# Three-stage attention and feed-forward kernel: weight words of the second phase loaded ahead of their conversions, scratch stores behind the loads

## Chip, cores, metric

One core of a Trainium2 chip. The metric is the device time of one execution in microseconds (us); lower is better. Half a per cent of it is 2.6 us.

## Reference

Three stages in fp32, on 2 x 768 = 1536 tokens of 512 features:

```python
# 1: attention, 8 heads of 64; a window of +-15 keys, and 24 block summaries (max of k, mean of v over 32)
a = softmax(concat(where(near, q @ k.T / 8, -1e9), q @ ksum.T / 8 + log(32)))
x = a @ concat(v, vsum)                       # as [1536, 512]
# 2: feed-forward 512 -> 1024 -> 512
h = x @ w_in
s = h * softmax(h)
x = (s - mean(s)) / sqrt(var(s) + 1e-6) * g_ln @ w_out
# 3: feed-forward 512 -> 2048 -> 512, elu
h = x @ w_in2
out = where(h > 0, h, exp(min(h, 0)) - 1) @ w_out2
```

The weights reach the kernel as 64-bit words (two 32-bit words per number), so each one is converted to fp32 on the chip, and then split into a high and a low part. A product is three matmuls: high times high, high times low, low times high (L103 to L105).

## The kernel before, in words

The program has two phases. **The first** runs stage 1 and stage 2 as one loop over 24 "ticks" (`ticks`): in each, one tile of 64 tokens enters attention (`attn_s`), others are further on (`attn_p`, `attn_x`), half of a product with `w_in` is done for 128 tokens (`mm_in`), and, as they come ready, transposes (`tr`, into `lnT`) and products with `w_out` (`mm_out(i, d)`, 24 matmuls for 384 tokens and 128 features, L103 to L105 with `y_ps`). Behind the ticks stand `mm_out` of the third and of the fourth block of 384 tokens, with the last three transposes. `mm_out` leaves its result in PSUM; ACT copies it into the three tiles `y` of 512 tokens each (L305), and the blocks of 384 don't meet the tiles of 512: a result of the third block goes in part to the second tile and in part (128 tokens) to the third.

**The second phase** is stage 3. First the first 512 tokens: 16 blocks `f` of 128 hidden features, each `ffn2_in(f)` (12 matmuls, `h2`, then the elu and its split into `g_hl`) and, one block behind, `ffn2_out` (12 matmuls into `o_ps`). Then the other 1024 tokens by products of sums (`yf`, `w3e`, `w3l`, `c11`, `c12`, `c21`).

The weights of stage 3 are converted in 32 pieces, 16 of `w_in2` (here ("w3", f)) and 16 of `w_out2` (("w4", f)), half a megabyte of words each. `todo` holds their order, and `more_w(n)` does the next n. One conversion is: a DMA of the words into a buffer (`load_words`, L112); Abs of the high words on ACT (L120); a clamp on POOL (L123); three VectorE steps (L124, L125, L129), of which L125 and L129 read the words too. A `w3` piece stays in SBUF. A `w4` piece is split (ACT L133, VectorE L100) and stored to scratch in DRAM (`store_w4`, L358, `w4d`), from where it is read back three times into the three buffers `w4r` (`load_w4`, L381).

The buffers for the words are pieces of the `y` tiles that don't hold results yet: `spare` is at first two halves of the third `y` tile (in the trace `y<-in_w_in`, in the order below `y2_67`). So the evacuations of `mm_out` into the third tile wait for the last conversions out of it. After the ticks one half of the first tile and two halves of another tile take their place.

All DMAs are issued from SP's queue, which runs in order; while the first phase lasts, their order on SP is that of the program. In `more_w` a `w3` or `w4` piece is loaded, in program order, just ahead of its own conversion, and the stores of earlier pieces are issued ahead of that (`store_w4()` stands before each `more_w`). The order on the other engines is made by a scheduler, also in order at run time; only on TensorE, in the products of sums, it is the program's.

Of the kernel before, what the change touches and what calls it, by code (L numbers as in the profile page):

```python
# [9 lines left out]
F32 = mybir.dt.float32  # L10
F32R = mybir.dt.float32r
BF16 = mybir.dt.bfloat16
I32 = mybir.dt.int32
# [19 lines left out]
TC = 512  # L33
KD, KF1, KF2 = DM // 128, F1 // 128, F2 // 128
# [17 lines left out]
def tile_kernel(ctx: ExitStack, tc: tile.TileContext, qd, kT, v, w_in, w_out, g_ln, w_in2, w_out2,  # L52
# [4 lines left out]
    state = {"late": 0}  # L57
# [10 lines left out]
    stage = [[t.bitcast(I32)[:, i * 1024:(i + 1) * 1024].rearrange("p (k f) -> p k f", k=KD)  # L68
              for i in range(KD * TC // 1024)] for t in flat]

    p_c = ctx.enter_context(tc.tile_pool(name="p_c", bufs=1, side="right"))
    p_ln = ctx.enter_context(tc.tile_pool(name="p_ln", bufs=1, side="right", reuse_waits="tile"))
# [15 lines left out]
    dump = p_ln.tile([128, F1], BF16, tag="dump", name="dump")  # L88
# [22 lines left out]
    def load_words(bits, src):  # L111
        nc.sync.dma_start(bits, src if len(src.shape) == 3 else src.rearrange("p (k f) -> p k f", k=KD))  # L112
# [19 lines left out]
    def split(hi, lo, x):  # L132
        nc.scalar.activation(hi, x, AF.Copy)  # L133
        lo_of(lo, x, hi)

    def convert(bits, src, hi, lo, g=None, pin=False):
        if src is not None:
            load_words(bits, src)
        hi, lo = (t if len(t.shape) == 3 else t.rearrange("p (k f) -> p k f", k=KD) for t in (hi, lo))
        x = to_f32(bits, pin=pin)  # L140
        if g is None:
            split(hi, lo, x)
        else:
            nc.scalar.activation(hi, x, AF.Copy, scale=g)
            nc.vector.scalar_tensor_tensor(lo, x, g, hi.bitcast(F32), op0=ALU.mult, op1=ALU.subtract)
# [45 lines left out]
    def load_v(n):  # L191
        b, t = divmod(n, NT)
        nc.sync.dma_start(vws[n % NBUF][0:WIN, :], v[b, t * TQ:t * TQ + WIN, :])
# [101 lines left out]
    def ffn1_out(i, d, k):  # L295
# [4 lines left out]
        if k == KF1 - 1:  # L300
# [6 lines left out]
                t0 = t1  # L307

    w3t, w3e, w3l, w3_hl, w4s, w4_hl, yhl, yf = {}, {}, {}, {}, {}, {}, {}, {}
    stores, spare = [], [*stage[2]]  # L310
    todo = [("w3", 0), ("w3", 1), ("w4", 0), ("w3", 2), ("w3", 3), ("w4", 1), ("w3", 4), ("w3", 5), ("w4", 2),
            ("w4", 3), ("w3", 6), ("w4", 4), ("w3", 7), ("w4", 5), ("w3", 8), ("w4", 6), ("w3", 9), ("w4", 7),
            ("w4", 8), ("w4", 9)]
    todo += [("w3", f) for f in range(10, KF2)] + [("w4", f) for f in range(10, KF2)]

    def bits():
        state["late"] += 1
        return spare[state["late"] % len(spare)]

    def home(p):  # L320
        if p < 2:
# [10 lines left out]
    def base_of(f):  # L332
        return w3f(f // 2)[:, 2:6:3] if f % 2 else w3f(f // 2)[:, 0:4:3]

    def convert_w3(f):
        b = bits()
        load_words(b, w_in2[:, f * 128:(f + 1) * 128].bitcast(I32).rearrange("(k p) f -> p k f", p=128))
        if f % 2 == 0:
            home(f // 2)
        to_f32(b, base_of(f).bitcast(I32))  # L340
# [5 lines left out]
        nc.vector.tensor_tensor(t[:, 1], t[:, 4], t[:, 0], op=ALU.subtract)  # L346
        nc.vector.tensor_tensor(t[:, 6], t[:, 3], t[:, 1], op=ALU.subtract)

    def convert_w4(f):
        t = w4s[f % 2]  # L350
        tr_ = t.bitcast(F32R)
        convert(bits(), w_out2[f * 128:(f + 1) * 128, :].bitcast(I32), tr_[:, 0], tr_[:, 1])
        stores.append((f, t))

    def store_w4():
        while stores:
            f, t = stores.pop(0)
            nc.sync.dma_start(w4d[f], t.rearrange("p c f -> p (c f)"))  # L358

    def more_w(n=1):  # L360
        for _ in range(n):
            if todo:
                what, f = todo.pop(0)
                (convert_w3 if what == "w3" else convert_w4)(f)

    def plain_w3(f):
        if f < KF2:
# [119 lines left out]
    late = {**dict.fromkeys(range(11, 21), 1), 21: 2, 22: 2, 23: 2}  # L487
    for t, (j, n) in enumerate(ticks):
        s_n, p_n, x_n = t + LEAD, t + LEAD - 2, t + LEAD - 3
        if t == 0:  # L490
            sum_v(1)
        elif t == 1:
            load_k(1)
        elif t == 3:
            sum_k(1)
        if x_n < NU and t:
            load_v(x_n)
        if s_n < NU:
            for u in (s_n + 1, s_n):
                if u < NU and u not in q_bd:  # L500
                    load_q(u)
            load_kw(s_n + 1)
            attn_s(s_n)
        mm_in(j, n)
        if p_n < NU:
            attn_p(p_n)
        for f, *args in after[t]:
            f(*args)
        if x_n < NU:
            attn_x(x_n)  # L510
        for _ in range(fetches.get(t, 0)):
            words.pop(0)()
        for _ in range(converts.get(t, 0)):
            parts.pop(0)()
        store_w4()
        more_w(late.get(t, 0))
        if x_n == NU - 1:
            p_at.release()
            p_w3 = ctx.enter_context(tc.tile_pool(name="p_w3", bufs=1, side="left", reuse_waits="tile"))
            for f in (3, 4):  # L520
                w3t[f] = p_w3.tile([128, 2048], F32, tag=f"f{f}", name="w3f")
            w3e[0] = p_w3.tile([128, 2, 3, 2, 128], F32R, name="w3e")
            last_t = p_w3.tile([128, 2, KF1, TB], F32R, tag="last", name="lnT")
            lnT_last = [last_t[:, c] for c in range(2)]
    p_in.release()
    p_y = ctx.enter_context(tc.tile_pool(name="p_y", bufs=1, side="right", reuse_waits="tile"))
    for d in range(KD):
        mm_out(NJ // 3 - 2, d)
        store_w4()
        if d == 2:  # L530
            split_y(0)
            spare[:] = stage[0][:1]
            mids = [stage[0][1].bitcast(F32).rearrange("p k f -> p (k f)")[:, c * TC:(c + 1) * TC] for c in range(2)]
            more_w()
        if d < 3:
            tr(NJ - 3 + d)
    tb = p_y.tile([128, 2, KD, 256], I32, tag="yc", name="bits")
    spare.extend(tb[:, c] for c in range(2))
    gw = p_w.tile([128, 6, 2, TC], F32R, tag="lnT", name="g_hl")
    wt = p_ln.tile([128, 5, 2, TC], F32R, tag="ln", name="w4r")  # L540
    w4r = [wt[:, c] for c in range(3)]
    w3h = [(t[:, 0], t[:, 1]) for t in (gw[:, 4], gw[:, 5], wt[:, 3], wt[:, 4])]
    for d in range(KD):
        mm_out(NJ // 3 - 1, d)
        store_w4()
        more_w()
        if d > 1:
            plain_w3(d - 2)
    store_w4()
    psh.release()  # L550
    loads.__exit__(None, None, None)
    mids.append(p_ln.tile([128, TC], F32, tag="dump", name="m"))

    pso = ctx.enter_context(tc.tile_pool(name="pso", bufs=4, space=PSUM))
    NTT = TC // 128
# [49 lines left out]
        load_w4(n)  # L605
    ops = tiles_o()
    for f in range(KF2):
        more_w(2)
        store_w4()
        ffn2_in(f)  # L610
        plain_w3(f + 2)
        for t in range(NTT):
            if f:
                ffn2_out(ops, t, f - 1)
        load_w4(f + 2)
        if f == 9:
            t4 = forms_early()
        if f == 12:
            sums_w3(0)
            w3l[0] = p_w.tile([128, 2, 4, 2, 128], F32R, tag="w3", name="w3l")  # L620
            split_w3(0)
            sums_w3(1)
# [23 lines left out]
    for p in range(NP3):  # L646
# [33 lines left out]
        pool, tag = ((p_k, "k") if p < 2 else (p_k, "f2") if p == 2 else (p_w3, f"f{p}") if p < 5 else (p_w, f"w{p - 5}"))  # L680
# [72 lines left out]
```

## Time and profile before

| | us |
|---|---|
| median of 3 runs | 520.16 (518.06 to 520.97) |
| the profiled execution | 520.19 |
| its span, first to last instruction | 518.4 |
| PE (TensorE matmul) busy | 471.9, 91% |
| DVE (VectorE) busy | 330.0, 64% |
| ACT busy | 287.7, 55% |
| POOL busy | 125.8, 24% |
| DMA, mean share of the 16 engines | 48.6% for SP's queue |

The profile is of one execution. A row of its timelines gives the start of an instruction in us from the span's start, its length, engine, line, operation and tiles, and in brackets how long its engine was idle before it and which instruction released it. Matmuls overlap their neighbours: a row's length is more than the spacing of two. The time of the runs is some 1.8 us more than the span.

### The profile page before, as it was taken

The numbers are of one execution on the slowest core, as the hardware profiler recorded it, in microseconds if no ns is written. First come the engines' busy times: TensorE is split into PE (matmuls) and PEld (weight loads), VectorE is DVE, ScalarE is ACT, GpSimd is POOL, SyncE is SP. The second block draws the span as 40 slices with busy tenths as digits, with TensorE's granted clock in tenths as the row PEclk, the third lists the DMA queues.
The fourth block names the chain that finished last, engine by engine and source line by source line (L and its number), as shares of the span: only waits on it lengthen the run. The fifth ranks groups of instructions, "written<-read, shape, count | busy, mean of one in ns | idle before, by whom it ended". The sixth has DMA issues, their size and how long they took to land.

```text
span 518.4 us, 7444 instructions
## 1 busy us (share of the span) xinstructions
PE 471.9 (91%) x2568; PEld 393.2 (76%) x2568; DVE 330.0 (64%) x759; ACT 287.7 (55%) x635; POOL 125.8 (24%) x198
## 2 busy tenths in 40 slices
PE   0988999999999998709999999779999999999997
PEld 1555888889978988709988887558888888888885
DVE  2798879978693769453565699977666666442000
ACT  1776888965773466232554648547766667551001
POOL 2886555872335313110000132300000000000000
PEclk9999999999999999868999999989999999999999
DMA  8986994262444223733347557574211212227654
GB/s 293 364 287 188 283 287 136 61 183 91 148 135 152 66 85 109 243 123 93 111 130 258 180 168 227 213 262 144 82 54 68 82 41 82 82 82 242 196 185 148
DMA packets 40117, 82.47 MB, mean 159 GB/s; under 512 B 9616, under 2 KB 18448, under 8 KB 40080
## 3 DMA queue, kind: packets, MB, share of 16 engines
q1 hardware_dynamic: 40080, 82.00, 48.6%
q8 instruction: 20, 0.33, 0.3%
q14 instruction: 17, 0.14, 0.1%
HBM read 70.46 MB, written 11.53 MB: 158 GB/s over the span
## 4 chain that ended last, share of the span: by engine, by line
PE 64%; DVE 14%; DMA 9%; issue 5%; ACT 3%; POOL 2%; SPq 1%; ACTq 0%; POOLq 0%; DVEq 0%
PE o_ps L105 6%; PE o_ps L104 6%; PE o_ps L103 6%; PE c L104 5%; PE c L105 5%; PE c L103 5%; PE h L103 5%; PE h L105 4%; PE h L104 4%; PE s_ps L213 3%; PE y_ps L103 3%; PE y_ps L104 3%; PE y_ps L105 3%; DMA y<-in_w_in 3%; PE x_ps L249 3%
## 5 line engine op out<-in xcount | busy, mean ns | idle before, releaser
L123 POOL TENSOR_SCALAR conv<-conv 128x512 f32<-128x512 f32 x48 | 40.0, 836 | 136.5 <-ACT conv L120 135.1
L103 PE MATMUL y_ps<-lnT,w_out 128*128 128x384 f32 x128 | 45.1, 353 | 16.2 <-ACT y L305 12.8
L103 PE MATMUL o_ps<-w4r,g_hl 128*128 128x512 f32 x128 | 50.9, 397 | 6.6 <-DMA w4r<-w4d 6.6
L227 POOL TENSOR_SCALAR sm<-sm,st 128x120 f32<-128x120 f32 x96 | 47.6, 513 | 28.6 <-DVE st L225 13.0
L104 PE MATMUL o_ps<-w4r,g_hl 128*128 128x512 f32 x128 | 50.6, 395 | 0.0
L120 ACT ACTIVATE conv<-y 128x512 f32<-128x512 f32 x38 | 25.4, 672 | 44.7 <-DMA y<-in_w_in 33.3
L105 PE MATMUL o_ps<-w4r,g_hl 128*128 128x512 f32 x128 | 48.2, 395 | 0.0
L104 PE MATMUL y_ps<-lnT,w_out 128*128 128x384 f32 x128 | 44.6, 350 | 0.0
L105 PE MATMUL y_ps<-lnT,w_out 128*128 128x384 f32 x128 | 44.5, 350 | 0.0
L124 DVE TENSOR_SCALAR conv<-conv 128x512 int32<-128x512 int32 x48 | 22.3, 464 | 29.7 <-POOL conv L123 29.7
L103 PE MATMUL h<-w_in,xT 128*128 128x512 f32 x96 | 40.2, 419 | 0.8 <-ACT xT L252 0.8
L213 PE MATMUL s_ps<-kw,q_bd 128*128 128x120 f32 x192 | 28.7, 296 | 12.6 <-DMA q_bd<-in_qd 11.7
L105 PE MATMUL h<-w_in,xT 128*128 128x512 f32 x96 | 38.7, 403 | 0.5 <-DVE xT L100 0.5
L222 ACT ACTIVATE sm<-sm,st 128x120 f32<-128x120 f32 x96 | 36.8, 387 | 4.2 <-DVE st L219 2.7
L104 PE MATMUL h<-w_in,xT 128*128 128x512 f32 x96 | 38.3, 399 | 0.6 <-DVE w_in L100 0.6
L103 PEld LDWEIGHTS y_ps<-lnT,w_out 128*128 128x128 f32 x128 | 25.4, 199 | 17.3 <-ACT y L305 13.2
L213 PEld LDWEIGHTS s_ps<-kw,q_bd 128*128 128x128 f32 x192 | 25.1, 203 | 13.9 <-POOL kw L96 11.6
L103 PEld LDWEIGHTS o_ps<-w4r,g_hl 128*128 128x128 f32 x128 | 24.5, 191 | 13.7 <-issue 3.3
L592 DVE COPY y<-o_ps 128x512 f32<-128x512 f32 x5 | 3.4, 689 | 43.5 <-PE o_ps L105 43.5
L594 ACT ACTIVATE y<-o_ps 128x512 f32<-128x512 f32 x6 | 3.6, 598 | 45.1 <-PE o_ps L105 45.1
L105 PEld LDWEIGHTS o_ps<-w4r,g_hl 128*128 128x128 f32 x128 | 24.5, 191 | 5.2
L104 PEld LDWEIGHTS o_ps<-w4r,g_hl 128*128 128x128 f32 x128 | 24.3, 190 | 5.0
(151 smaller groups left out, 1268.2 us busy)
## 6 DMA issues: line engine op xcount, KB each, us to landing
w4r<-w4d SPq DMA_DIRECT2D x48, 512.0 KB, 4.2
y<-in_w_in SPq DMA_DIRECT2D x20, 512.0 KB, 6.2
y<-in_w_out SPq DMA_DIRECT2D x18, 512.0 KB, 5.2
w4d<-w3f SPq DMA_DIRECT2D x16, 512.0 KB, 3.5
q_bd<-in_qd SPq DMA_DIRECT2D x24, 256.0 KB, 6.1
vw<-in_v SPq DMA_DIRECT2D x24, 192.0 KB, 5.7
k_sb<-in_kT SPq DMA_DIRECT2D x8, 400.0 KB, 5.2
v_sb<-in_v SPq DMA_DIRECT2D x12, 256.0 KB, 6.0
```

The source lines that it names most:

```text
L103: nc.tensor.matmul(ps, lhsT=l[0][ls], rhs=r[0][rs], start=first, stop=False, skip_group_check=parts)
L104: nc.tensor.matmul(ps, lhsT=l[0][ls], rhs=r[1][rs], start=False, stop=False, skip_group_check=parts)
L105: nc.tensor.matmul(ps, lhsT=l[1][ls], rhs=r[0][rs], start=False, stop=last, skip_group_check=parts)
L120: first = nc.scalar.activation(x, high.bitcast(F32), AF.Abs)
L123: nc.gpsimd.tensor_scalar(x, x, F64_HUGE, F64_TINY, op0=ALU.min, op1=ALU.max)
L124: nc.vector.tensor_scalar(a, a, 3, 0x3FFFFFF8, op0=ALU.logical_shift_left, op1=ALU.bitwise_and)
L213: nc.tensor.matmul(sps[:, p, 0:KW], lhsT=q_bd[n][:, p, :], rhs=kw[:, p, :], start=True, stop=True)
L222: nc.scalar.activation(sm[:, p, :], sm[:, p, :], AF.Exp, bias=nm[:, p:p + 1], scale=-1.0, accum_out=ss[:, p:p + 1])
L227: nc.gpsimd.tensor_scalar(sm[:, p, :], sm[:, p, :], ri[:, p:p + 1], 1.0, op0=ALU.mult, op1=ALU.mult)
L249: nc.tensor.matmul(xps[ds, p, :], lhsT=vw[:KW, p * 128 + hh * D:p * 128 + (hh + 1) * D], rhs=pT[:KW, p, hh * TQ:(hh + 1) * TQ], start=True ...
L592: nc.vector.tensor_copy(o, ops[t])
L594: nc.scalar.activation(o, ops[t], AF.Copy)
```

## The change

- `fetch()` is new: it loads the words of the next pieces of `todo` as long as fewer than `len(spare) - 1` are waiting for their conversion (`ahead`). It is called first in the tick before the first conversion, then at the head of each `more_w`. With the two buffers of the first phase one load is ahead, with the four later ones three.
- `more_w` now calls `fetch()`, then `store_w4()`, then does the oldest piece of `ahead`. A store of a `w4` piece therefore stands behind the next load. The separate calls of `store_w4` are gone.
- The later buffers are four halves of two tiles (`yc`, `yd`), taken from the second output tile (d = 1) of the third block of 384 tokens on; the first `y` tile holds none any more, and its four quarters are scratch for the elu (`mids`).
- In the third block of 384 tokens two pieces are converted instead of one, in the fourth four as before. In the first 512 tokens of the second phase `more_w()` does one piece per block of 128 features instead of two, and `todo` alternates there between `w4` and `w3`.
- `forms_early` (sums of the other tokens, which take the tiles `yc` and `yd`) stands after block 11 instead of 9.

```diff
-    stores, spare = [], [*stage[2]]
+    stores, ahead, spare = [], [], [*stage[2]]
     todo = [("w3", 0), ("w3", 1), ("w4", 0), ("w3", 2), ("w3", 3), ("w4", 1), ("w3", 4), ("w3", 5), ("w4", 2),
             ("w4", 3), ("w3", 6), ("w4", 4), ("w3", 7), ("w4", 5), ("w3", 8), ("w4", 6), ("w3", 9), ("w4", 7),
-            ("w4", 8), ("w4", 9)]
-    todo += [("w3", f) for f in range(10, KF2)] + [("w4", f) for f in range(10, KF2)]
-
-    def bits():
-        state["late"] += 1
-        return spare[state["late"] % len(spare)]
+            ("w4", 8), ("w4", 9), ("w3", 10), ("w3", 11)]
+    for f in range(10, KF2):
+        todo += [("w4", f)] + [("w3", f + 2)] * (f + 2 < KF2)
+
+    def fetch():
+        while todo and len(ahead) < len(spare) - 1:
+            what, f = todo.pop(0)
+            b = spare[state["late"] % len(spare)]
+            state["late"] += 1
+            if what == "w3":
+                load_words(b, w_in2[:, f * 128:(f + 1) * 128].bitcast(I32).rearrange("(k p) f -> p k f", p=128))
+            else:
+                load_words(b, w_out2[f * 128:(f + 1) * 128, :].bitcast(I32))
+            ahead.append((what, f, b))
...
     def more_w(n=1):
         for _ in range(n):
-            if todo:
-                what, f = todo.pop(0)
-                (convert_w3 if what == "w3" else convert_w4)(f)
+            fetch()
+            store_w4()
+            if ahead:
+                what, f, b = ahead.pop(0)
+                (convert_w3 if what == "w3" else convert_w4)(f, b)
...
-        store_w4()
+        if t == min(late) - 1:
+            fetch()
         more_w(late.get(t, 0))
...
+    tb = [p_y.tile([128, 2, KD, 256], I32, tag=n, name="bits") for n in ("yc", "yd")]
     for d in range(KD):
         mm_out(NJ // 3 - 2, d)
-        store_w4()
+        more_w(d > 1)
+        if d == 1:
+            spare[:] = [t[:, c] for c in range(2) for t in tb]
+            state["late"] = 0
+            fetch()
         if d == 2:
             split_y(0)
-            spare[:] = stage[0][:1]
-            mids = [stage[0][1].bitcast(F32).rearrange("p k f -> p (k f)")[:, c * TC:(c + 1) * TC] for c in range(2)]
-            more_w()
+            mids = [stage[0][h].bitcast(F32).rearrange("p k f -> p (k f)")[:, c * TC:(c + 1) * TC]
+                    for h in range(2) for c in range(2)]
...
     for f in range(KF2):
-        more_w(2)
-        store_w4()
+        more_w()
         ffn2_in(f)
...
-        if f == 9:
+        if f == 11:
             t4 = forms_early()
```

What this does to the order on SP, at the end of the ticks (`y2_67` is the third `y` tile as a buffer, `w4d5_101` the scratch of ("w4", 5)). Before:

```order
L358 DMA w4d4_100<-w3f_1367 128x1024
L112 DMA y2_67<-in_w_in2 128x4x256
L112 DMA y2_67<-in_w_out2 128x1024
L381 DMA w4r_2478<-w4d0_96 128x1024
L381 DMA w4r_2478<-w4d1_97 128x1024
L381 DMA w4r_2478<-w4d2_98 128x1024
L358 DMA w4d5_101<-w3f_1650 128x1024
L112 DMA y2_67<-in_w_in2 128x4x256
L112 DMA y2_67<-in_w_out2 128x1024
```

With the change (`bits` are the new buffers):

```order
L112 DMA y2_67<-in_w_in2 128x4x256
L364 DMA w4d4_100<-w3f_1367 128x1024
L112 DMA y2_67<-in_w_out2 128x1024
L112 DMA y2_67<-in_w_in2 128x4x256
L364 DMA w4d5_101<-w3f_1650 128x1024
L112 DMA y2_67<-in_w_out2 128x1024
L112 DMA bits_2312<-in_w_in2 128x4x256
L112 DMA bits_2313<-in_w_out2 128x1024
L112 DMA bits_2312<-in_w_out2 128x1024
L389 DMA w4r_2490<-w4d0_96 128x1024
L389 DMA w4r_2490<-w4d1_97 128x1024
L389 DMA w4r_2490<-w4d2_98 128x1024
```

Each load now stands ahead of the store that it stood behind, and the last two loads into the third `y` tile (L112 ahead of the first `bits` row) ahead of the three reads of `w4r`.

On ACT, the same place in the program, from the copies of the last 384 tokens' first transposes on (`lnT_2155`; `conv_2253` is ("w3", 7), `conv_2293` ("w3", 8), `conv_2300` ("w4", 6)). Before:

```order
L290 ACTIVATE lnT_2155<-t_ps_2381 128x4x128
L290 ACTIVATE lnT_2155<-t_ps_2388 128x4x128
L133 ACTIVATE w3f_1367<-conv_2216 128x512
L305 ACTIVATE y1_66<-y_ps_2395 128x256
L290 ACTIVATE lnT_2155<-t_ps_2435 128x4x128
L120 ACTIVATE conv_2253<-y2_67 128x512
L290 ACTIVATE lnT_2155<-t_ps_2442 128x4x128
L120 ACTIVATE conv_2260<-y2_67 128x512
L133 ACTIVATE w4r_2478<-w3f_1650 128x512 x2
L305 ACTIVATE y1_66<-y_ps_2449 128x256
L133 ACTIVATE g_hl_2477<-w3f_1367 128x512 x2
L133 ACTIVATE w3f_1650<-conv_2260 128x512
```

With the change:

```order
L290 ACTIVATE lnT_2155<-t_ps_2385 128x4x128
L290 ACTIVATE lnT_2155<-t_ps_2392 128x4x128
L120 ACTIVATE conv_2293<-y2_67 128x512
L133 ACTIVATE w3f_1650<-conv_2260 128x512
L305 ACTIVATE y1_66<-y_ps_2399 128x256
L290 ACTIVATE lnT_2155<-t_ps_2439 128x4x128
L305 ACTIVATE y2_67<-y_ps_2314 128x128
L305 ACTIVATE y2_67<-y_ps_2355 128x128
L290 ACTIVATE lnT_2155<-t_ps_2446 128x4x128
L133 ACTIVATE w4r_2490<-w3f_1650 128x512 x2
L120 ACTIVATE conv_2300<-y2_67 128x512
L120 ACTIVATE conv_2427<-bits_2312 128x512
```

The Abs of ("w3", 8) moved from behind the evacuation of `y_ps_2449` to ahead of that of the tile before, and two evacuations into the third tile now stand ahead of the last transposes' copy.

On ACT earlier, at the end of the first phase (`conv_2140` is ("w4", 3), `conv_2209` ("w3", 6), `conv_2216` ("w4", 4)). Before:

```order
L305 ACTIVATE y0_65<-y_ps_2100 128x128
L305 ACTIVATE y1_66<-y_ps_2100 128x256
L252 ACTIVATE xT_2064<-x_ps_2127 128x4x64
L120 ACTIVATE conv_2140<-y2_67 128x512
L290 ACTIVATE lnT_94<-t_ps_2179 128x4x128
L290 ACTIVATE lnT_94<-t_ps_2186 128x4x128
L270 ACTIVATE ln_95,st_2168<-h_2087,st_2168 128x1024
```

With the change:

```order
L120 ACTIVATE conv_2209<-y2_67 128x512
L305 ACTIVATE y0_65<-y_ps_2100 128x128
L305 ACTIVATE y1_66<-y_ps_2100 128x256
L252 ACTIVATE xT_2064<-x_ps_2127 128x4x64
L120 ACTIVATE conv_2216<-y2_67 128x512
L290 ACTIVATE lnT_94<-t_ps_2179 128x4x128
L290 ACTIVATE lnT_94<-t_ps_2186 128x4x128
```

Each Abs stands one conversion earlier than before among the same evacuations and copies.

## Rows read from the trace of the kernel before

**Rows 1.** Stretches: from:to, length; PE, PEld, DVE, ACT, POOL busy (count); granted clock; DMA share.

```profile
203.00:220.50 17.50, 12.75 (x66) 11.66 (x65) 9.96 (x17) 5.94 (x11) 3.04 (x4) 0.90 0.52 180
220.50:233.40 12.90, 0.05 (x2) 0.05 (x1) 7.19 (x14) 4.49 (x9) 1.69 (x2) 0.66 0.36 123
233.40:239.80 6.40, 6.40 (x24) 6.40 (x25) 1.98 (x3) 1.03 (x4) 0.00 (x0) 0.62 0.44 141
239.80:252.60 12.80, 12.80 (x75) 12.80 (x74) 5.59 (x10) 3.34 (x6) 1.23 (x2) 1.00 0.17 54
252.60:322.00 69.40, 69.40 (x308) 57.48 (x307) 50.99 (x91) 41.85 (x72) 10.79 (x13) 1.00 0.58 185
322.00:350.00 28.00, 20.97 (x80) 15.35 (x78) 25.12 (x33) 14.97 (x23) 5.14 (x2) 0.94 0.70 245
```

**Rows 2.** Timeline of PE (start, length, engine, line, operation, tiles, [idle before <-releaser]).

```profile
233.35 0.69 PE L103 MATMUL y_ps<-lnT,w_out 128*128 128x384 f32 x1 [12.85 <-ACT y L305]
```

**Rows 3.** Timeline of ACT, before and in the long wait.

```profile
213.84 0.67 ACT L120 ACTIVATE conv<-y 128x512 f32<-128x512 f32 x1 [0.62 <-DMA y<-in_w_in]
...
229.37 0.66 ACT L120 ACTIVATE conv<-y 128x512 f32<-128x512 f32 x1 [4.30 <-DMA y<-in_w_in]
...
233.03 0.45 ACT L305 ACTIVATE y<-y_ps 128x128 f32<-128x128 f32 x2 [1.79 <-DVE w3f L129]
```

**Rows 4.** Timeline of SP's queue (DMA issues), 180 to 225.

```profile
180.32 0.34 SPq L358 DMA_DIRECT2D w4d<-w3f  x1
...
193.65 0.39 SPq L112 DMA_DIRECT2D y<-in_w_in  x1
...
207.30 0.33 SPq L358 DMA_DIRECT2D w4d<-w3f  x1
207.68 0.43 SPq L112 DMA_DIRECT2D y<-in_w_in  x1
...
214.73 1.28 SPq L381 DMA_DIRECT2D w4r<-w4d  x3
223.89 0.32 SPq L358 DMA_DIRECT2D w4d<-w3f  x1
224.25 0.43 SPq L112 DMA_DIRECT2D y<-in_w_in  x1
```

**Rows 5.** Timeline of DVE: last read of ("w3", 7), split of ("w4", 5).

```profile
218.49 0.68 DVE L129 SCALAR_TENSOR_TENSOR w3f<-y,conv 128x512 int32<-128x512 int32 x1
...
223.19 0.68 DVE L100 TENSOR_TENSOR w3f<-conv,w3f 128x512 fp32r<-128x512 f32 x1
```

**Rows 6.** Waits of PE, 247 to 352 (waiting <- releaser: total, times, longest).

```profile
PE o_ps L103 <- DMA w4r<-w4d: 6.6, 4, 2.5
```

**Rows 7.** Timeline of SP's queue, a late store and a reload.

```profile
327.30 0.32 SPq L358 DMA_DIRECT2D w4d<-w3f  x1
331.36 0.32 SPq L381 DMA_DIRECT2D w4r<-w4d  x1
```

**Rows 8.** The page's DMA issues (count, KB each, median us to landing).

```profile
y<-in_w_in SPq DMA_DIRECT2D x20, 512.0 KB, 6.2
```

**Rows 9.** Timeline of PE behind the last wait for w4r.

```profile
341.21 0.63 PE L105 MATMUL o_ps<-w4r,g_hl 128*128 128x512 f32 x1
341.64 0.63 PE L103 MATMUL o_ps<-w4r,g_hl 128*128 128x512 f32 x1
```

**Rows 10.** Timeline of ACT, first phase's end.

```profile
165.74 0.66 ACT L120 ACTIVATE conv<-y 128x512 f32<-128x512 f32 x1 [2.84 <-DMA y<-in_w_in]
...
186.34 1.09 ACT L290 ACTIVATE lnT<-t_ps 128x512 fp32r<-128x512 f32 x2 [0.90 <-PE t_ps L288]
```

**Rows 11.** Timeline of PE behind a short gap.

```profile
206.13 0.44 PE L103 MATMUL y_ps<-lnT,w_out 128*128 128x384 f32 x1 [1.92 <-DVE lnT L100]
...
208.01 0.53 PE L103 MATMUL y_ps<-lnT,w_out 128*128 128x384 f32 x1
208.33 0.53 PE L104 MATMUL y_ps<-lnT,w_out 128*128 128x384 f32 x1
```

More of the change, by code (lines that the diff above doesn't have):

```diff
@@ L333, in base_of, with convert_w3 @@
         return w3f(f // 2)[:, 2:6:3] if f % 2 else w3f(f // 2)[:, 0:4:3]
-    def convert_w3(f):
-        b = bits()
-        load_words(b, w_in2[:, f * 128:(f + 1) * 128].bitcast(I32).rearrange("(k p) f -> p k f", p=128))
+    def convert_w3(f, b):
         if f % 2 == 0:
@@ L347, in sums_w3, with convert_w4 @@
         nc.vector.tensor_tensor(t[:, 6], t[:, 3], t[:, 1], op=ALU.subtract)
-    def convert_w4(f):
+    def convert_w4(f, b):
         t = w4s[f % 2]
         tr_ = t.bitcast(F32R)
-        convert(bits(), w_out2[f * 128:(f + 1) * 128, :].bitcast(I32), tr_[:, 0], tr_[:, 1])
+        convert(b, None, tr_[:, 0], tr_[:, 1])
         stores.append((f, t))
@@ L526, in tile_kernel @@
     p_y = ctx.enter_context(tc.tile_pool(name="p_y", bufs=1, side="right", reuse_waits="tile"))
+    tb = [p_y.tile([128, 2, KD, 256], I32, tag=n, name="bits") for n in ("yc", "yd")]
     for d in range(KD):
         mm_out(NJ // 3 - 2, d)
-        store_w4()
+        more_w(d > 1)
[3 more added lines that the diff above has]
+            fetch()
         if d == 2:
             split_y(0)
-            spare[:] = stage[0][:1]
-            mids = [stage[0][1].bitcast(F32).rearrange("p k f -> p (k f)")[:, c * TC:(c + 1) * TC] for c in range(2)]
-            more_w()
+            mids = [stage[0][h].bitcast(F32).rearrange("p k f -> p (k f)")[:, c * TC:(c + 1) * TC]
+                    for h in range(2) for c in range(2)]
         if d < 3:
             tr(NJ - 3 + d)
-    tb = p_y.tile([128, 2, KD, 256], I32, tag="yc", name="bits")
-    spare.extend(tb[:, c] for c in range(2))
     gw = p_w.tile([128, 6, 2, TC], F32R, tag="lnT", name="g_hl")
@@ L548, in tile_kernel @@
             plain_w3(d - 2)
-    store_w4()
     psh.release()
     loads.__exit__(None, None, None)
-    mids.append(p_ln.tile([128, TC], F32, tag="dump", name="m"))
     pso = ctx.enter_context(tc.tile_pool(name="pso", bufs=4, space=PSUM))
@@ L607, in tile_kernel @@
     for f in range(KF2):
-        more_w(2)
-        store_w4()
+        more_w()
         ffn2_in(f)
```

## The prediction

> **What bounds the kernel now.** I read four views in this order: the busy time by stretch, the waits of TensorE, the timeline of each engine that released the longest wait, and the timeline of SP's queue.
>
> TensorE is busy for 91% of the span, so only the stretches where it isn't can give anything. [rows 1] cuts the middle of the span into such stretches. From 203.0 to 220.5 it is idle for 4.75 us (17.50 less 12.75) in short pieces; from 220.5 to 233.4 it stands still; from 233.4 to 239.8 it runs without a gap, but 24 matmuls take 6.40 us where the next stretch needs 12.80 us for 75, or 0.171 us each; from 252.6 to 322 it is saturated, with 308 matmuls in 69.4 us, or 0.225 us each; from 322 to 350 it is idle for 7.03 us (28.00 less 20.97). After 350 it is busy again but for the last output. So the price on offer lies in two places, and the question is what ends last in each.
>
> The long wait is 12.85 us before the first matmul of the last block's second output tile [rows 2]. Its releaser is the evacuation of an older tile into `y` (L305). That evacuation writes words 0 to 127 of the third `y` tile, which until then are the raw weight buffers, so it may run only when the last words there are converted. ACT's rows show it [rows 3]: the Abs of ("w3", 8) waits 4.30 us for its DMA, ACT then waits 1.79 us for VectorE's last read, and the evacuations follow at 233.03. Why was that DMA late? SP's rows [rows 4]: its load was issued only at 224.25, directly behind a store at 223.89, which had waited for the split of ("w4", 5) on VectorE, 223.19 to 223.87 [rows 5]. The words that this load overwrites were those of ("w3", 7), free since 219.17 (the first of [rows 5]); and that load had itself gone out at 207.68, behind the store of 207.30. So SP is a queue in which a store that waits for a conversion holds the next load.
>
> The second place is four waits of together 6.6 us for w4r [rows 6]. SP again [rows 7]: the last `w4` blocks are stored at 327.30 and later, and each reload follows its store by about 4 us. The weights are late because two conversions were asked for per block of 128 features and their loads came one at a time.
>
> **The change part by part.** (1) In the first phase the load of conversion n+1 now precedes the store of conversion n. There are still two buffers there, so one load is ahead; [rows 4] says what this frees. ("w3", 6) may be loaded once the store at 180.32 is out, instead of at 193.65, 13 us earlier. Each later link is a landing plus a conversion behind other work. A landing of `w_in2` words is 6.2 us in the median [rows 8]; I take 6, then Abs, POOL and three VectorE steps, about 3 us. With the VectorE order as now written, ("w3", 6) is last read near 196, ("w3", 7) goes out near 196 (before: 207.68) and is read by 205, ("w3", 8) goes out near 205 (before: 224.25) and is read near 214. The three w4r loads, which waited at 214.73 for the last transposes, no longer stand ahead of it. ("w4", 6) follows the store of ("w4", 5), near 212, and is read near 221. The evacuation that needs it is wanted only after two further output tiles of 24 matmuls, 8.2 us at 0.171, behind a tile that ends near 221, so near 229. The 12.85 us go.
>
> (2) With that wait goes the low clock after it: [rows 1] gives a granted clock of 0.62 in that stretch, between the levels 2.4 and 1.2 GHz, after TensorE had done nothing for 12.85 us. 24 matmuls at 0.171 would be 4.1 us instead of 6.4: 2.3 us.
>
> (3) The second phase. Four buffers of a tile apart hold three loads ahead; one conversion per block from 22 already done; stores behind loads. The last `w4` conversion now stands in block 9, six blocks (24 matmuls, 5.4 us each) ahead of its product. All four w4r waits should go: 7.03 us idle, and seven matmuls at a spacing of 0.43 instead of 0.225 us [rows 9], 1.4 us. Together 8.4; by counting matmuls in [rows 1] it is 28.0 less 80 times 0.225, or 10.0. I take 8.4, since a few records can be missing.
>
> (4) What is moved at no price: each conversion costs the same instructions as before, and nothing is added but another buffer tile. VectorE was busy 81.7 us from 239.8 to 350 in three rows of [rows 1], and TensorE's matmuls of the same stretch need 12.8 + 69.4 + 18.0 = 100.2 us, so the cover holds if the work starts on time; the forms of the second and third token block move from blocks 10 and on to 12 and on, because their tiles are buffers until block 9. If VectorE falls behind in blocks 0 to 8, where all ten conversions are, TensorE waits for a split; I count 1 us for that, 0 to 4.
>
> (5) What it costs. ACT's Abs instructions stand one conversion earlier among the attention and normalisation work. ACT runs in order, so an Abs whose words haven't landed holds what is behind it. In the trace such waits are 2.84 us at most in this stretch, at 165.74, and TensorE had other work; but the one at ("w4", 4) now stands just ahead of the copy of the transposed tile that began at 186.34 [rows 10], with TensorE waiting for it soon after. I count 1.5 us there, and nothing for the others; the bounds are 0 and 2.84 at two places, 5.7 us.
>
> What the clock makes of a new wait is open. A gap of 1.92 us at 204.2 was followed from 207.5 by ten matmuls at a spacing of 0.32 instead of 0.171 us [rows 11], 1.5 us lost, while two gaps of 1.41 us at 212 to 216 had no such price. [...]
>
> Sum: 12.85 + 2.3 + 8.4 = 23.6 off; 1 + 1.5 + 1.5 on (the last for one more gap at the price of [rows 11], by the row alone) = 4. Net 19.6. The profiled execution took 520.19 us, 1.8 more than its span, and the median of the runs is 520.16, so either base serves: 520.2 less 19.6 is 500.6. I round it down to **500**, since the other count in (3) takes off 1.6 us more.
>
> **The rivals.** *The wait only moves.* Four tiles of PSUM stand open for the last block; the second transposes of the last 128 tokens, at 214 before, now take the place that ("w3", 8) frees. If the chain of three links runs 2.7 us later at each, because more loads are in flight, the wait comes at 214 and is 8 us long: 508. For it: the load of 224.25, with one more behind it, took 5.1 us to its Abs, that of 207.68, with a store ahead of it as well, 6.2 [rows 3, 4]. The Trainium skill (DMA: Bandwidth & Descriptors, Issuing engines are not separate DMA queues) has all transfers interleave on the same engines, which makes landings longer with more ahead; the trace agrees. Against: each link has been given 9 us. 0.12.
>
> *VectorE becomes the bound in blocks 0 to 8*, and half of part (3) comes back: 504. It is inside my range, and I count it with the forecast.
>
> *Slower: ACT waits for words all through the first phase's end.* Six Abs, those of ("w3", 4), ("w4", 3), ("w3", 6), ("w4", 4), ("w3", 7) and ("w3", 8), now stand ahead of work that TensorE needs. If each load went out only when its Abs was reached, each would cost the 6.2 us of [rows 8], 37 us, and the time would be 520.2 - 23.6 + 37 = 534. It turns slower from 3.9 us each (23.6 over 6). Against: each load is earlier by one conversion too, and 2.84 us is the longest such wait there. 0.05.
>
> *Nothing happens*, since with two buffers a load still waits for the conversion two before it: 518 to 522. Against: the loads of 207.68 and 224.25 waited for stores, not for buffers. 0.03.
>
> **How the numbers follow.** The forecast, 494 to 505, has 0.8. Its lower end is all of 12.85 + 2.3 + 10.0 and no new wait (495), and a little of the 4.75 us from 203 to 220.5; its upper end has 5.7 and 4 us of new waits. To hold 8 in 10 the range reaches to the first rival: 494 to 508. Half a per cent, 2.6 us, is about what a measurement of this kernel can tell from no change. Faster by more than that: 0.92 (forecast and first rival); same 0.03; slower 0.05.
>
> **What would show it.** Right: no TensorE wait over 3 us from 200 to 340; the load of ("w3", 8) out by 207; no wait of o_ps for w4r; the first matmul of the second phase near 238 (before: 252.58); the first product of the third stage less than 90 us behind it. Wrong: a TensorE wait of over 5 us for `t_ps` or `y_ps` near 214, or several of 2 us or more from 155 to 200 whose releaser is ACT behind an Abs.

## The result and the profile after

The changed kernel took **497.19 us** (median of 4, 496.84 to 498.08) where the kernel before took 520.57 (median of 4, 518.06 to 521.53): a ratio of 0.9561, with an interval of 0.9524 to 0.9597. The forecast was 500, with a range of 494 to 508. The profiled execution was the longest of its four (498.08, span 496.3), so 22.1 us of span are to be found against the 23.4 of the medians.

The stretches of [rows 1] in the profile after, in the same columns (the same times of the span; the work in them has moved forward):

```profile
203.00:220.50 17.50, 13.60 (x74) 13.06 (x73) 12.96 (x26) 8.05 (x19) 4.24 (x5) 0.90 0.52 185
220.50:233.40 12.90, 12.90 (x75) 12.90 (x74) 12.10 (x22) 7.84 (x17) 3.03 (x4) 1.00 0.87 314
233.40:239.80 6.40, 6.40 (x38) 6.40 (x38) 5.82 (x11) 2.98 (x7) 2.54 (x2) 1.00 0.77 262
239.80:252.60 12.80, 12.80 (x59) 10.71 (x58) 11.77 (x20) 11.42 (x20) 3.71 (x4) 1.00 0.64 221
252.60:322.00 69.40, 69.40 (x308) 57.47 (x307) 56.90 (x91) 39.08 (x64) 9.48 (x7) 1.00 0.58 196
322.00:350.00 28.00, 28.00 (x125) 23.06 (x124) 19.38 (x27) 19.72 (x33) 0.00 (x0) 1.00 0.28 97
```

The second row is the long wait: 0.05 us of TensorE before, 12.90 now, and the third has no low clock. The last had 7.03 us of idle time and now has none. VectorE is busy for 88.1 us in the last three rows (11.77 + 56.90 + 19.38), all of it beside a TensorE that doesn't stop for 110.2 us. What TensorE still waits for, from the list of its waits over the whole span (waiting <- releaser: total, times, longest):

```profile
PE s_ps L213 <- POOL kw L96: 12.4, 1, 12.4
PE y_ps L103 <- DVE lnT L100: 3.0, 1, 3.0
PE h L103 <- ACT xT L252: 1.6, 3, 0.8
...
PE s_ps L213 <- ACT vsum L185: 0.9, 1, 0.9
PE t_ps L288 <- ACT y L305: 0.9, 1, 0.9
```

The first is the start of the program; what is left out is 1.3 us or less. No wait for an evacuation by `y_ps` and none for `w4r` is left. SP's queue shows why the first of these is gone, where [rows 4] showed the store holding the load:

```profile
200.17 0.38 SPq L112 DMA_DIRECT2D y<-in_w_in  x1
200.60 0.50 SPq L364 DMA_DIRECT2D w4d<-w3f  x1
...
209.64 0.38 SPq L112 DMA_DIRECT2D y<-in_w_in  x1
215.29 0.33 SPq L364 DMA_DIRECT2D w4d<-w3f  x1
```

The load of ("w3", 7) goes out at 200.17, ahead of a store (before: 207.68), that of ("w3", 8) at 209.64 (before: 224.25), and the store of ("w4", 5) stands behind both. What SP waited for, before (195 to 230) and after (195 to 220), the longest of each:

```profile
SPq L358 <- DVE w3f L100: 12.2, 1, 12.2
```

```profile
SPq L112 <- DVE w3f L129: 23.0, 2, 15.0
```

The store no longer holds these loads; they go out as VectorE's last read of the words that they overwrite ends (for the load of 209.64, at 209.58). So they are now held by the two buffers. ACT, in the places of [rows 3]:

```profile
204.41 0.67 ACT L120 ACTIVATE conv<-y 128x512 f32<-128x512 f32 x1 [0.80 <-DMA y<-in_w_in]
...
206.96 0.70 ACT L120 ACTIVATE conv<-y 128x512 f32<-128x512 f32 x1 [1.60 <-DMA y<-in_w_out]
...
208.93 1.09 ACT L290 ACTIVATE lnT<-t_ps 128x512 fp32r<-128x512 f32 x2
213.33 0.68 ACT L120 ACTIVATE conv<-y 128x512 f32<-128x512 f32 x1 [3.31 <-DMA y<-in_w_in]
...
226.59 0.43 ACT L305 ACTIVATE y<-y_ps 128x128 f32<-128x128 f32 x2
```

The Abs of ("w3", 8) starts at 213.33 instead of 229.37, and the last words leave the third `y` tile in time for the evacuation of 226.59, which nobody waits for. TensorE around the one gap that is left there, and at the start of the second phase:

```profile
211.57 0.67 PE L103 MATMUL y_ps<-lnT,w_out 128*128 128x384 f32 x1 [3.04 <-DVE lnT L100]
212.03 0.52 PE L104 MATMUL y_ps<-lnT,w_out 128*128 128x384 f32 x1
212.35 0.52 PE L105 MATMUL y_ps<-lnT,w_out 128*128 128x384 f32 x1
...
240.45 0.39 PE L103 MATMUL h<-y_hl,g_hl 128*128 128x512 f32 x1
```

The gap of 3.04 us is longer than the 1.92 before, and matmuls behind it stand 0.32 us apart, as in [rows 11]. There the granted clock is 0.50, the level of 1.2 GHz (from 212.0 to 214.9; 1.00, or 2.4 GHz, from 215.2 on); such a stretch is called a slow spell below. The second phase starts at 240.45 (before: 252.58), so 12.13 us come from the first phase; from there to the end it is 255.85 us (496.3 less 240.45) instead of 265.82, so 9.97 from the second.

### The profile page after: what moved, and what is told of

The parts are those of the page before. It is cut to its first block, busy times and chain, and to the rows that moved or that the text cites. A ratio compares the mean times of both kernels' runs of the same rounds, so it can differ in the third digit from the quotient of the medians.

```text
span 496.3 us, 7444 instructions
## 1 busy us (share of the span) xinstructions
PE 469.2 (95%) x2568; PEld 391.9 (79%) x2568; DVE 330.3 (67%) x759; ACT 288.2 (58%) x635; POOL 125.5 (25%) x198
## 4 chain that ended last, share of the span: by engine, by line
PE 81%; DVE 6%; DMA 5%; ACT 3%; POOL 2%; issue 1%; SPq 0%; POOLq 0%; ACTq 0%
PE o_ps L103 8%; PE o_ps L105 8%; PE o_ps L104 8%; PE h L103 7%; PE h L105 7%; PE h L104 6%; PE c L105 5%; PE c L103 5%; PE c L104 5%; PE y_ps L103 4%; PE y_ps L105 4%; PE y_ps L104 4%; PE s_ps L213 3%; DMA y<-in_w_out 3%; PE x_ps L249 2%; DMA k_sb<-in_kT 1%
## 5 line engine op out<-in xcount | busy, mean ns | idle before, releaser
L103 PE MATMUL o_ps<-w4r,g_hl 128*128 128x512 f32 x128 | 49.8, 389 | 0.0
L104 PE MATMUL o_ps<-w4r,g_hl 128*128 128x512 f32 x128 | 49.8, 389 | 0.0
L105 PE MATMUL o_ps<-w4r,g_hl 128*128 128x512 f32 x128 | 45.6, 389 | 0.0
L120 ACT ACTIVATE conv<-y 128x512 f32<-128x512 f32 x32 | 21.5, 675 | 31.5 <-DMA y<-in_w_in 23.7
L572 ACT ACTIVATE y<-y 128x512 f32<-128x512 f32 x48 | 30.1, 629 | 0.8
L100 DVE TENSOR_TENSOR g_hl<-y,g_hl 128x512 fp32r<-128x512 f32 x32 | 22.4, 700 | 9.3 <-ACT g_hl L133 9.3
L103 PEld LDWEIGHTS o_ps<-w4r,g_hl 128*128 128x128 f32 x128 | 24.0, 188 | 5.1
```

Of the source, the lines that this page charges most:

```text
L100: nc.vector.tensor_tensor(out_, x, hi.bitcast(F32), op=ALU.subtract)
L103: nc.tensor.matmul(ps, lhsT=l[0][ls], rhs=r[0][rs], start=first, stop=False, skip_group_check=parts)
L104: nc.tensor.matmul(ps, lhsT=l[0][ls], rhs=r[1][rs], start=False, stop=False, skip_group_check=parts)
L105: nc.tensor.matmul(ps, lhsT=l[1][ls], rhs=r[0][rs], start=False, stop=last, skip_group_check=parts)
L120: first = nc.scalar.activation(x, high.bitcast(F32), AF.Abs)
L572: nc.scalar.activation(m, m, AF.Exp, scale=-1.0)
```

## The experiments

Three questions: what freed the first phase, what freed the second, and what the new waits cost. All kernels ran beside the kernel before; times are medians, ratios are to that kernel.

**Store ahead of load again.** The changed kernel, with two lines exchanged:

```diff
-            fetch()
             store_w4()
+            fetch()
```

> The changed kernel with the store put ahead of the fetch again; buffers, order of the pieces and number ahead stay as changed. Theory A (in the first phase the order of store and load on SP is what counts): the wait of TensorE for an evacuation into the third y tile is back with 8 to 13 us and a low clock behind it, the first matmul of the second phase comes at 249 to 253, and with the second phase still about 10 us shorter the total is 505 to 511, 508 the likeliest. Theory B (the two new buffers, free from the third block's second output tile on, are what counts): no such wait, 496 to 499.

Measured: 512.21 us, ratio 0.9822 (0.9777 to 0.9867). SP's queue and TensorE (two places):

```profile
224.42 0.32 SPq L364 DMA_DIRECT2D w4d<-w3f  x1
224.79 0.43 SPq L112 DMA_DIRECT2D y<-in_w_in  x1
```

```profile
233.84 0.69 PE L103 MATMUL y_ps<-lnT,w_out 128*128 128x384 f32 x1 [8.71 <-ACT y L305]
234.33 0.52 PE L104 MATMUL y_ps<-lnT,w_out 128*128 128x384 f32 x1
...
252.40 0.40 PE L103 MATMUL h<-y_hl,g_hl 128*128 128x512 f32 x1
```

The store of 224.42 again holds the load of ("w3", 8), to within 0.6 us of where [rows 4] had it, the wait is back with 8.71 us and a slow spell behind it (granted clock 0.50 from 233.9 to 237.4), and the second phase starts at 252.40. So the order of two calls decides the first phase. The second phase keeps its gain, 255.6 us. The median is a little above the range of theory A (505 to 511), the profiled execution, 509.93, within it; theory B falls.

**Load ahead of store, alone.** The kernel before, where in the ticks a store is now issued behind the next load:

```diff
-        store_w4()
+        if not late.get(t):
+            store_w4()
         more_w(late.get(t, 0))
...
         load_words(b, w_in2[:, f * 128:(f + 1) * 128].bitcast(I32).rearrange("(k p) f -> p k f", p=128))
+        store_w4()
```

(and likewise in the conversion of a `w4` piece).

> The kernel before with one thing changed: in the ticks of the first phase a store is issued behind the next load instead of ahead of it. Theory A: the long wait goes, the first matmul of the second phase comes at 239 to 243 (before: 252.58), the four waits for w4r of together 6 to 7 us stay, total 506 to 511, 508 the likeliest (520.2 less 12.2). Theory B: the long wait stays at 10 us or more, total 518 to 521.

Measured: 515.57 us, ratio 0.9901 (0.9866 to 0.9935): a miss for the sum, though the mechanism is there. TensorE, SP's queue, and TensorE's waits for w4r from 238 to 360:

```profile
238.72 0.39 PE L103 MATMUL h<-y_hl,g_hl 128*128 128x512 f32 x1
...
321.55 0.79 PE L103 MATMUL o_ps<-w4r,g_hl 128*128 128x512 f32 x1 [8.94 <-DMA w4r<-w4d]
322.14 0.63 PE L104 MATMUL o_ps<-w4r,g_hl 128*128 128x512 f32 x1
```

```profile
206.53 0.38 SPq L112 DMA_DIRECT2D y<-in_w_in  x1
...
224.44 0.32 SPq L362 DMA_DIRECT2D w4d<-w3f  x1
224.81 0.43 SPq L112 DMA_DIRECT2D y<-in_w_in  x1
```

```profile
PE o_ps L103 <- DMA w4r<-w4d: 12.5, 2, 8.9
```

("w3", 8) goes out at 206.53, the long wait is gone, and the second phase starts at 238.72, 13.9 us earlier than before. Then 10.8 of it are lost again in the profiled execution (517.13 us): the second phase takes 276.6 us, with 12.5 us of waits for w4r instead of 6.6 and a spacing of 0.43 us behind the longest. The last Abs of any words, before and in this run, shows how far the conversions reach:

```profile
328.34 0.66 ACT L120 ACTIVATE conv<-bits 128x512 f32<-128x512 f32 x1
```

```profile
328.59 0.66 ACT L120 ACTIVATE conv<-bits 128x512 f32<-128x512 f32 x1 [1.23 <-DMA bits<-in_w_out]
```

The chain of conversions ends when it ended before, and TensorE only comes sooner to wait for it. So the two gains don't add up from their parts: the first-phase edit alone gives 5.3 us (520.83 less 515.57), the rest alone 8.6 (520.83 less 512.21), and both together 23.4 (from the medians of the result).

**What shortens the second phase.** Five parts are looked at here: the order of store and load, the loads ahead, one conversion per block, the order of the last pieces, and the buffers. Two more parts, the two conversions in the third block of 384 tokens and the later place of `forms_early`, are in every changed kernel below and were taken out of none. The first run above took the order away, without effect. The next takes away the rate, with the old order of the last pieces:

```diff
-        more_w()
+        more_w(2)
         ffn2_in(f)
```

> The changed kernel with two conversions per block of 128 features and the old order of the last pieces (all w3, then w4); three loads ahead stay. Theory A (depth of loads ahead is what took the waits for w4r away): no wait of o_ps for w4r over 1 us, total 496 to 499. Rival (one conversion per block in alternating order is what took them away): waits of 3 to 7 us and a low clock behind the last, total 501 to 507.

Measured: 495.67 us, ratio 0.9517 (0.9476 to 0.9557), no wait for w4r, 255.7 us. The rate does nothing. Then the number of loads ahead:

```diff
-        while todo and len(ahead) < len(spare) - 1:
+        while todo and len(ahead) < 1:
```

> The changed kernel with one load at a time in the second phase too (four buffers, one conversion per block, stores behind loads as changed). With the order of the store (its place ahead of the load left the second phase at 255.6 us) and the rate (two per block left it at 255.7) both without effect, theory A is left with the depth: a landing of 4 to 6 us then stands in every block of 5.4 us on ACT, ahead of the elu; from the first matmul of the second phase to the end 258 to 266 us instead of 255.9, total 500 to 508. Rival (four buffers in two tiles of their own are enough, the depth does nothing): 255 to 257 us, total 496 to 499.

Measured: 496.25 us, ratio 0.9532 (0.9511 to 0.9552), 255.5 us. My theory that the depth does it fell with this run. A new one took its place, that the buffers do it, and two runs tried it from both sides. In the one the new buffers stand alone but for those two parts, with all the other rules of before (the exchange, the rate, the old order of pieces, and one load at a time, as in the diffs above):

> Only the four new buffers, taken from the third block's second output tile on, and the two conversions there: store ahead of load, one load at a time, two conversions per block and the old order of the last pieces, as in the kernel before. Theory F (the second phase is decided by how many pieces are converted by its first matmul, and so by buffers that come free before the evacuations; the order, the depth and the rate do nothing there): the wait for the evacuation is back (7 to 13 us), the second phase takes 255 to 258 us instead of 265.8, total 509 to 514. Rival (order, depth and rate each would have done alone, and with all three gone the waits for w4r are back): the second phase takes 262 us or more, total 516 to 521.

Measured: 517.90 us, ratio 0.9950 (0.9928 to 0.9972), second phase 262.6 us: the rival's numbers. TensorE's waits from 254 to 360, and ACT's last Abs:

```profile
PE o_ps L105 <- DVE g_hl L100: 1.7, 2, 1.4
PE c L104 <- DVE yf L100: 1.1, 1, 1.1
PE o_ps L103 <- ACT g_hl L133: 0.7, 2, 0.4
```

```profile
317.93 0.68 ACT L120 ACTIVATE conv<-bits 128x512 f32<-128x512 f32 x1 [0.50 <-DVE w3f L100]
```

VectorE was busy for 39.49 of the 40 us from 290 to 330 there.

In the other the new rules stand, with the old buffers (and so with one load ahead, later two; the line of `fetch` for that is not shown):

```diff
-        if d == 1:
-            spare[:] = [t[:, c] for c in range(2) for t in tb]
-            state["late"] = 0
-            fetch()
         if d == 2:
             split_y(0)
+            spare[:] = stage[0][:1]
...
+    tb = p_y.tile([128, 2, KD, 256], I32, tag="yc", name="bits")
+    spare.extend(tb[:, c] for c in range(2))
```

> The changed kernel with the buffers of the second phase as before: one half of the first tile from the third block's third output tile on, then two halves of another tile as well; order, rate and depth (one, later two loads ahead) as changed. Theory F: first matmul of the second phase at 238 to 242, waits for w4r of together 5 to 13 us, second phase 262 us or more, total 503 to 514. Rival (the new order of loads and the rate are enough): no wait for w4r over 1 us, total 496 to 499.

Measured: 495.24 us, ratio 0.9510 (0.9484 to 0.9536), no wait for w4r, 255.6 us, with the last Abs at

```profile
292.09 0.66 ACT L120 ACTIVATE conv<-bits 128x512 f32<-128x512 f32 x1 [1.74 <-DMA bits<-in_w_out]
```

So that theory falls too, on both sides: the new buffers aren't needed. What orders all the runs is how far the chain of conversions reaches into the second phase (starts from the profiles, in us; the last two columns are for the first 40 us of the phase: VectorE's busy time, and how long SP waited for TensorE's product, `o_ps`, ahead of a reload of w4r):

| kernel | first matmul of the phase | last Abs | behind it | phase | VectorE busy | SP for `o_ps` |
|---|---|---|---|---|---|---|
| load first alone | 238.7 | 328.6 | 89.9 | 276.6 | 23.93 | 20.0 |
| before | 252.6 | 328.3 | 75.7 | 265.8 | 22.96 | 13.1 |
| buffers alone | 254.4 | 317.9 | 63.5 | 262.6 | 27.65 | 10.3 |
| old buffers, new rules | 235.8 | 292.1 | 56.3 | 255.6 | 36.75 | 7.6 |
| one load at a time | 239.7 | 291.3 | 51.6 | 255.5 | 34.37 | 5.0 |
| two per block | 238.4 | 277.9 | 39.5 | 255.7 | 38.32 | 7.3 |
| changed | 240.5 | 278.9 | 38.4 | 255.8 | 37.95 | 2.0 |
| store first | 252.4 | 290.0 | 37.6 | 255.6 | 37.13 | 3.5 |

Up to 56 us it costs nothing (the other kernels of the study, at 35 to 42 us, have phases of 255.5 to 256.8), and from 63 us on the phase grows with it. That is a common measure of the runs, not a cause shown by itself. Order, depth or rate may each be taken away; with all three and the new order of the last pieces gone the chain is late again, with the new buffers by waits for VectorE rather than for w4r. Whether one of the three alone would do was not tried.

The first 80 us of the phase before, and the first 40 after (columns as in [rows 1]), show what a late chain means for VectorE:

```profile
252.58:292.58 40.00, 40.00 (x178) 33.13 (x178) 22.96 (x37) 22.43 (x39) 3.18 (x5) 1.00 0.51 171
292.58:332.58 40.00, 37.68 (x166) 30.58 (x165) 38.61 (x70) 27.25 (x47) 11.97 (x9) 1.00 0.66 212
```

```profile
240.45:280.45 40.00, 40.00 (x178) 33.12 (x178) 37.95 (x67) 27.57 (x48) 13.03 (x11) 1.00 0.74 258
```

Before, VectorE is idle for 17 of the first 40 us and then nearly full (38.61 of 40) while TensorE comes to wait; after, it is nearly full from the start (37.95) and TensorE doesn't wait. The three late kernels are the three with the least VectorE work in the first 40 us, and the three in which SP waited longest ahead of a reload. Loads of words stand behind these reloads in SP's queue, as they stood behind the stores in the first phase, so the reloads may be what makes the chain late. No run moved them: this cause is not shown.

**What the new waits cost.** The profile after had the last product of the attention (L249) at 187.0, before 182.7, and I took the 4.3 us for ACT waiting for words. In the changed kernel `fetch` leaves room for one piece and `more_w` takes it in the same call: from the second piece of the first phase on, a load stands just ahead of its own conversion. (That one load is ahead there, as the section on the change has it, holds for the first piece alone.) This edit makes it true:

```diff
-            fetch()
+            piece = ahead.pop(0) if ahead else None
+            fetch()
             store_w4()
-            if ahead:
-                what, f, b = ahead.pop(0)
+            if piece:
+                what, f, b = piece
```

and `fetch` stops at 16 pieces in the third `y` tile, so that nothing more is loaded there.

> The changed kernel, but a piece is taken before the next is fetched, so that in the first phase a load really is issued one conversion ahead (in the changed kernel, where one may wait and is taken in the same call, a load stands just ahead of its own conversion). Theory C (the 4 us that the changed kernel loses before 187 us are ACT waiting for words): the last product of the attention comes at 182 to 185 instead of 187.0, ACT's idle time for words from 100 us on falls from 23 us to under 12, total 492 to 495. Rival (they come from the order of VectorE's and ACT's work, not from late words): the last product of the attention at 186 or later, total 496 to 500.

Measured: 493.84 us, ratio 0.9488 (0.9439 to 0.9537). The time is that of theory C, its reason isn't: ACT's idle time for words from 100 us on is 23.3 us, as in the changed kernel (22.8). So the two were run side by side.

> The changed kernel once more, beside the next one on the same chip: 496 to 498. If the 4.3 us by which the last product of the attention came later than before (187.0 against 182.7) belong to the change, it is at 186 to 188 again; if most of them differ from one execution to the next (the kernel with two conversions per block has the same instructions in the same order up to there and had 183.8), it is at 183 to 185.

> The kernel whose loads are really one conversion ahead in the first phase, once more. Theory (its gain is of the shorter gap of TensorE near 207 and the low clock that then stays out, 3 us): 2 to 4.5 us less than the changed kernel on the same chip. Rival (the difference was that of two sessions): within 1 us of it.

The changed kernel took 497.28 us (ratio 0.9551, 0.9532 to 0.9569), and now its last product of the attention came at 183.7: most of the 4.3 us was that one execution's (about 1.5 of it a slow spell behind 156.9, which this execution didn't have). The other took 495.14 (0.9512, 0.9491 to 0.9534), 2.1 less, intervals that just meet. TensorE near 208, first the changed kernel, then the other:

```profile
208.93 0.69 PE L103 MATMUL y_ps<-lnT,w_out 128*128 128x384 f32 x1 [3.24 <-DVE lnT L100]
209.42 0.52 PE L104 MATMUL y_ps<-lnT,w_out 128*128 128x384 f32 x1
209.74 0.52 PE L105 MATMUL y_ps<-lnT,w_out 128*128 128x384 f32 x1
```

```profile
207.38 0.44 PE L103 MATMUL y_ps<-lnT,w_out 128*128 128x384 f32 x1 [1.92 <-DVE lnT L100]
207.66 0.34 PE L104 MATMUL y_ps<-lnT,w_out 128*128 128x384 f32 x1
```

A gap of 3.24 us against one of 1.92, and behind the first 16 matmuls at a spacing of 0.32 us where full speed has 0.174, 2.3 us in all; behind the second none. Of the 2.6 us by which its second phase starts sooner (236.2 against 238.8), these two make 3.6, and a longer wait for an evacuation (2.41 us near 215 instead of 0.86) takes 1.6 back.

> Both edits: loads really one conversion ahead in the first phase, and two conversions per block in the second phase. If the rate has no effect, within 1 us of the kernel without it. If earlier conversions in the first blocks crowd VectorE, 1 to 4 us more.

Measured: 493.58 us (0.9476, 0.9454 to 0.9497), clear of the changed kernel, not of the one with one conversion per block. It is 1.6 us less than that one, where 1 us was expected at most; the intervals overlap. The last two runs went after the remaining wait.

```diff
-    late = {**dict.fromkeys(range(11, 21), 1), 21: 2, 22: 2, 23: 2}
+    late = {**dict.fromkeys(range(11, 21), 1), 21: 2, 22: 2, 23: 1}
...
         mm_out(NJ // 3 - 1, d)
-        more_w()
+        more_w(2 if d == 0 else 1)
```

(and the limit of 16 pieces becomes 15)

> The kernel with loads really one ahead and two conversions per block, and one conversion moved from the last tick to the last block of 384 tokens, so that the third y tile holds words until one conversion earlier. If the wait of 2.4 us for an evacuation near 215 hangs on that conversion, it goes, and the total is 1 to 3 us below the kernel without this step; if it moves to another wait, within 1 us of it.

> The kernel with loads really one ahead and two conversions per block once more, beside the last one: 492.5 to 495.

Without the step 494.25 us (0.9499, 0.9474 to 0.9523), with it **492.23** (0.9453, 0.9426 to 0.9480). TensorE's wait and ACT's queue without it:

```profile
214.59 0.66 PE L288 MATMUL t_ps<-ident,ln 128*128 128x128 f32 x4 [2.45 <-ACT y L305]
```

```profile
212.96 0.66 ACT L120 ACTIVATE conv<-y 128x512 f32<-128x512 f32 x1 [2.97 <-DMA y<-in_w_out]
213.52 0.37 ACT L305 ACTIVATE y<-y_ps 128x256 f32<-128x256 f32 x1
```

ACT waits 2.97 us for the words of ("w4", 6) with the evacuations behind it in its queue. With the step the same wait of TensorE is

```profile
211.79 0.44 PE L288 MATMUL t_ps<-ident,ln 128*128 128x128 f32 x2 [0.20 <-ACT y L305]
```

Both are as expected, though the two intervals overlap. This is the best version of the study; its interval lies wholly below that of the changed kernel.

## Why the prediction was right

The time, the sign and the mechanism of the first phase held; two terms were mis-sized, and the independence of the two parts, which the sum took for granted, was not tested by it and doesn't hold.

- **Parts (1) and (2), 12.85 and 2.3 off, 3 on for (5) and one more slow spell.** Net 12.15 forecast for the first phase, 12.13 measured. That it meets to so little is luck: the second profile of the same kernel started the second phase at 238.8, 13.8 us earlier than before. The 0.62 read as a clock between the levels is an average: before, it was 0.50 from 233.4 to 238.0 and 1.00 from 238.3 on. The wait, its low clock and their cause are shown by the exchange of two lines, in both directions.
- **The dates of the chain** were early from the second link on. ("w3", 6) went out at 180.62, as forecast; ("w3", 7) was forecast out near 196 and came at 200.17, ("w3", 8) near 205 and came at 209.64, so "out by 207" was missed by 2.6 us. Landings were shorter than the 6 us taken (an Abs 4.2 us behind the load of 200.17, 3.7 behind that of 209.64); the links are longer behind the landing: the Abs of ("w3", 7) started at 204.41, and VectorE read its words for the last time at 208.89 to 209.58, behind other work. The slack at the end was enough.
- **Part (5)** had the right kind and the wrong place. Nothing was lost at the Abs of ("w4", 4): TensorE has no gap from 157 to 208. The price fell at 208.5, where ACT had waited 0.80 and 1.60 us for words ahead of the copy of the transposed tile. The copy began at 208.93, 0.40 us behind the end of the last transpose; before, and in the second run of the kernel with loads really ahead, it began 0.40 us ahead of that end, and the gap was 1.92 us in both. Here it was 3.04 us, just over the 3 us that the text set as a limit.
- **Part (3), 8.4 taken, 9.97 measured.** The second count of the text, 10.0, was the better one: it takes all the time of the stretch beyond 80 matmuls at 0.225 us, the first only the idle time and seven late matmuls. (In the second profile of the same kernel the phase was 256.5 us, 9.3 less than before.) The 1 us counted for VectorE wasn't paid either: TensorE has no wait for it in the phase, with VectorE busy for 37.95 of the first 40 us. These two, 1.6 and 1, are, to 0.1 us, the difference between 19.6 and 22.1 of span.
- **The step that failed as an argument** is the sum of (1) and (3) as if each could be had alone. "Three loads ahead", "one conversion per block" and "stores behind loads" were all named as the reason for (3); each alone can be taken away, and so can the buffers. And (1) alone is worth 5.3 us, not 12, since the late chain of (3) takes it back.
- **The rivals.** The wait did not move to the second transposes (0.86 us, at 218.89). The comparison given for that rival was misread: both loads, of 207.68 and of 224.25, stood 0.4 us behind a store and had another load half a microsecond behind them. They landed after 6.1 and 5.0 us, while a load of the same trace with no other near it (244.23, of `w_out2`) took 3.5. ACT idled 22.8 us for words from 100 us on, before 40.2, and no Abs of the six waited 3.9 us (3.31 at most, at 213.33). One more slow spell was counted, 1.5 us: in the profile after two gaps had one (behind 156.9 and behind 211.57), and in other runs gaps of about the same length had none.
- **The mark of 90 us** for the third stage was badly put: the first product with `w3l` came 91.2 us behind the first matmul of the phase (331.6 less 240.45; before: 101.5), which is the gain, but not "less than 90".

## What to carry to other kernels

In an in-order queue of DMAs, look at what each load stands behind: a store that waits for a computation holds every load after it. Here the exchange of two calls decided 2.6% of the time (a ratio of 0.9822 against 0.9561), and three loads ahead instead of one at a time decided nothing (0.9532 with one). A chain of loads and conversions that feeds two phases has one end; in this kernel the gain in the first phase was kept only where the chain ended early enough for the second, so cost the two together, by how far the chain reaches into the next phase, and look there for stretches in which the converting engine stands idle. And before explaining a few microseconds of one profile, run the same kernel again.

## What was not expected of the hardware

The same gap may or may not cost a slow spell. In the kernel before, 1.92 us at 206.13 were followed by ten matmuls at a spacing of 0.32 us [rows 11]; in the kernel with loads really ahead, 1.92 us at 207.38 by none. And in the run with the old buffers a longer gap had none either:

```profile
208.36 0.45 PE L103 MATMUL y_ps<-lnT,w_out 128*128 128x384 f32 x1 [2.87 <-DVE lnT L100]
208.64 0.34 PE L104 MATMUL y_ps<-lnT,w_out 128*128 128x384 f32 x1
```

The next matmul there follows after 0.28 us and the later ones after 0.17 to 0.18 (granted clock 1.00), while the changed kernel's 3.04 and 3.24 us had ten and 16 slow ones (0.50). It differs also between two executions of the same instructions: behind short gaps (0.64 and 0.16 us, near 156) the first profile of the changed kernel had ten matmuls at 0.32 us, the second none behind 0.63 and 0.16. Of such spells, 1.5 to 2.3 us each here, the length of the gap alone doesn't decide, and what does was not settled.
